# Residual sums shared between VectorE and GpSimd, the small product of the norm moved to VectorE, and a new order of all operations

## The chip, the cores and the metric

The kernel runs on one core of a Trainium2 chip. The metric is the device time of one execution in microseconds, the median of several runs. The engines are named as in the profile: PE (TensorE, matmuls), DVE (VectorE), ACT (ScalarE), POOL (GpSimd) and SP (SyncE, which issues all DMAs here).

## What is computed

The input x has 2048 rows of 448 bf16 values. Two blocks follow one another:

```python
x  = A_x
h  = x + attn(layernorm(x) @ wqkv) @ wo       # 16 heads of 28, causal window of 8 keys at steps of 2
y  = layernorm(h)
g  = gelu(layernorm(y) @ w1)                  # its four quarters shifted by -1, +1, -2, +2 rows
x1 = y + shifted(g) @ w2
out = h + (x1 + gelu(layernorm(x1) @ w3) @ w4)
```

The last line is the one that matters here: h, which lies in `xin`, has to be added to every row of x1 at the end, beside x1 itself.

## The kernel before

**Tiles and stages.** The 2048 rows are 16 tiles of 128. For the first half they are worked on in 4 groups of 4 tiles (512 rows), t = 0 to 3. Each goes through N1 (LayerNorm of x), A1 (transposed input times wqkv), V (values), A2 (logits with S, their softmax), A3 (weights times values, by way of block-diagonal factors `bd_r`), O (times wo, plus x: h), B1 (the two norms of h in one step, times w1, gelu) and M (its matmuls). The second half works in 5 units of 2, 4, 4, 4 and 2 tiles, u = 0 to 4: B2 (times w2, plus y: x1, called `xb`), T (LayerNorm of x1, made into `lntm` and turned by a transposing DMA into `actT`), W3 (times w3, gelu into `h3T`) and B3 (times w4, final sum, output). A letter with a number, such as T3 or W31, is a stage with its group or unit.

**Names.** `arena` is one large SBUF buffer; weights, q, k, g and the f32 rows `xb` lie in it, so that many rows of the profile have that name. `xin` holds x and then h (bf16). `lntm` are normalized rows, `mv` means and variances, `nm` negated means, `rs_x` variances and `rs_y` reciprocal standard deviations, `st` raw statistics, `pb`, `mx` and `ls` belong to the softmax, `ost` is the staging buffer of the output, `ps` a PSUM bank. `wo_s` holds wo, which comes in four DMAs.

**The end of a row.** y is never stored: y = h * rs_y - mean * rs_y. The B2 eviction (DVE, `scalar_tensor_tensor`) makes xb = h * rs_y + ps in f32. After T has read xb, the **residual sum** xb = xb + xin adds h (line 919-920, 16 times, one for each tile, on POOL). The **small product** mrs = nm * rs_y (line 547, four times, 128x4, on POOL) is the constant that is still missing in each row; the final eviction of B3 (line 944) computes ost = (ps + mrs) + xb on DVE. So neither the sum nor the product is needed before B3 of its tile.

**The order.** Every instruction is one of 858 operations, made by the phases and then sorted by a table of numbers, `ORDER` (line 22), which lists all of them: each engine executes its own operations in the order in which they stand there, strictly one after another. `OTHER` (line 53) lists the operations that take their alternative engine; most PSUM evictions have one (ACT or DVE). `arrange` (line 194) applies both and hands out buffers in that order from pools (8 PSUM banks, 3 `lntm`, 4 `actT`, 3 `bd_r`, 16 `h3T`, 5 `ost`): an operation waits for the last users of the buffer that it gets. `_emit_plan` (line 247) makes semaphore waits of the dependencies. POOL's queue holds set-up work, then `rs_y` as a power of `rs_x` where T takes it from there, the small products and the residual sums. SP's queue holds the DMAs: loads, copies of k and v between partitions (`arena<-arena`, `vw<-vt`), the transposes and the output.

Of the kernel before, what the change touches and what calls it, by code (L numbers as in the profile page):

```python
# [6 lines left out]
ALU = mybir.AluOpType  # L7
# [12 lines left out]
STAGE = '....'  # L20
ALONE = False
ORDER = """
# [29 lines left out]
"""  # L52
OTHER = """
91 94 114 187 188 501 507 549 550
"""
FULL = (4,)
FILL = (1, 1, 0, 0)
# [228 lines left out]
def bass_sequential_preLN__sliding_local_dilated__mixer_s_mlp__prompt_kernel(  # L286
# [16 lines left out]
    S = _Sched()  # L303
# [16 lines left out]
    with ExitStack() as es:  # L320
        def sb(name, shape, dt):
            return es.enter_context(nc.sbuf_tensor(name, shape, dt))
        AR = sb("arena", [128, A_END], BF16)
        xin = sb("xin", [128, NTL, D], BF16)
# [17 lines left out]
        rs_y = sb("rs_y", [128, 3, 2, NTL], F32)  # L342
        mrs = sb("mrs", [128, NTL], F32)
        nm = sb("nm", [128, 3, NTL], F32)
# [21 lines left out]
        def arv(off, parts, n):  # L366
            return AR[0:parts, off:off + n]
# [12 lines left out]
        xb = [arv(A_KV + i // 4 * KVB, 128, 4 * D * 2).bitcast(F32).rearrange("p (i d) -> p i d", d=D)[:, i % 4, :] for i in range(NTL)]  # L380
# [18 lines left out]
        def act(out_ap, in_ap, func, **kw):  # L399
            table = {ACT.Exp: "exp", ACT.Ln: "exp", ACT.Gelu_apprx_tanh: "gelu"}.get(func)  # L400
            return S.add("act", "activation", table=table, out=out_ap, in_=in_ap, func=func, **kw)
# [7 lines left out]
        def dve(meth, block=False, **kw):  # L409
            op = S.add("dve", meth, **kw)  # L410
            op.block = block
            return op

        def pool(meth, **kw):
            return S.add("pool", meth, **kw)
# [90 lines left out]
        def rstd(kind, i, m=4, summed=False, norms="v", how="p"):  # L506
            var = mv[:, kind, i:i + m, 1]
            by = 1.0 / D if summed else 1.0
            first = int(kind == 1)
            shifted_ = "a" in norms  # L510

            def power(k):
                S.add("pool", "tensor_tensor", out=rs_y[:, kind, k, i:i + m], in0=rs_x[:, kind, k, i:i + m], in1=mhalf[:, 0:m], op=ALU.pow)

            def power_act(k):
                act(rs_x[:, kind, k, i:i + m], var, ACT.Ln, scale=by * (1.0 + EPS * k), bias=epsilon[:, k:k + 1])
                act(rs_y[:, kind, k, i:i + m], rs_x[:, kind, k, i:i + m], ACT.Exp, scale=-0.5)

            def shift(k):
                if m == 1:  # L520
                    act(nmr[:, kind, i:i + 1], nm[:, kind, i:i + 1], ACT.Identity, scale=rs_y[:, kind, k, i:i + 1])
                else:
                    dve("tensor_tensor", out=nmr[:, kind, i:i + m], in0=nm[:, kind, i:i + m], in1=rs_y[:, kind, k, i:i + m], op=ALU.mult)

            if not summed and (shifted_ or kind == 1):
                dve("tensor_scalar", out=nm[:, kind, i:i + m], in0=mv[:, kind, i:i + m, 0], scalar1=-1.0, scalar2=None, op0=ALU.mult)
            if how == "a":
                power_act(first)
                if shifted_:
                    shift(first)  # L530
                if kind == 1:
                    power_act(0)
            else:
                if kind == 1:
                    dve("tensor_scalar", out=rs_x[:, kind, 1, i:i + m], in0=var, scalar1=by * (1.0 + EPS), scalar2=EPS * EPS, op0=ALU.mult, op1=ALU.add)
                    power(1)
                    if shifted_:
                        shift(1)
                if kind == 1 or summed:
                    dve("tensor_scalar", out=rs_x[:, kind, 0, i:i + m], in0=var, scalar1=by, scalar2=EPS, op0=ALU.mult, op1=ALU.add)  # L540
                else:
                    dve("tensor_scalar", out=rs_x[:, kind, 0, i:i + m], in0=var, scalar1=EPS, scalar2=None, op0=ALU.add)
                power(0)
                if kind != 1 and shifted_:
                    shift(0)
            if kind == 1:
                pool("tensor_tensor", out=mrs[:, i:i + m], in0=nm[:, 1, i:i + m], in1=rs_y[:, 1, 0, i:i + m], op=ALU.mult)

        CHUNK = (0, 128, 192, 320)

# [337 lines left out]
        def phase_B2(u):  # L888
# [28 lines left out]
            for n, i in enumerate(tiles):  # L917
                normalize(2, i, ln, n, xb[i], TURN["B2"][u], summed, norms[n])
            for i in tiles:
                S.add("pool", "tensor_tensor", out=xb[i], in0=xb[i], in1=xin[:, i, :], op=ALU.add).block = True  # L920
            b2_a[u] = transposed(ln, TURN["B2"][u], len(tiles))

        h3 = {}
# [129 lines left out]
```

## Time and profile before

| | us |
|---|---|
| median of 3 runs | 191.43 (191.26 to 191.53) |
| profiled execution | 191.99 |
| its span, first to last instruction | 190.3 |
| PE busy | 180.0 (95%), 2434 matmuls |
| DVE busy | 129.9 (68%) |
| ACT busy | 123.4 (65%) |
| POOL busy | 26.5 (14%) |

All instructions come from one line of the source, the emitting loop, so the profile's groups are told apart by the names of the tiles. A row of a timeline has the start, the length, the engine, the operation with output <- inputs, the number of instructions taken together and, in brackets, the idle time ahead of it with what ended it. A row SPq is a DMA's issue on SP's queue; the transfer goes on behind it. Matmul ends are modelled.

### The profile page before, as it was taken

What the parts mean: (1) busy time and instruction counts of PE and PEld (TensorE: products, weight loads), DVE (VectorE), ACT (ScalarE), POOL (GpSimd) and SP (SyncE); (2) the same over time, 40 slices, a digit from 0 to 9 for tenths busy, and PEclk for the clock granted to TensorE, in tenths of its full rate; (3) what the DMA queues carried; (4) which work ended last, traced back from release to release, by engine and by line L of the source; (5) the groups of instructions that cost most, each with busy time, mean ns of one, the idle gap of its engine ahead of it and who ended that gap; (6) DMA issues with size and microseconds to landing.
All of it is one profiled execution on the core that took longest, in us unless ns stands there. A gap on an engine that the chain in (4) does not pass through costs nothing.

```text
span 190.3 us, 5623 instructions
## 1 busy us (share of the span) xinstructions
PE 180.0 (95%) x2434; PEld 96.3 (51%) x2434; DVE 129.9 (68%) x226; ACT 123.4 (65%) x282; POOL 26.5 (14%) x61
## 2 busy tenths in 40 slices
PE   6699999897999989999989999999999999999994
PEld 2496433354443545565645535545444454455672
DVE  6999999999999999998998940099850006002203
ACT  3459999998999999999644897910256303650250
POOL 2250000000010000002205100181386002000000
DMA  5950254477407895796250060015044004000031
GB/s 147 339 193 3 44 110 110 78 174 158 103 3 114 160 272 225 136 331 134 50 113 0 5 134 0 3 30 108 0 91 119 0 0 112 19 3 0 17 109 48
DMA packets 36577, 18.06 MB, mean 95 GB/s; under 512 B 25304, under 2 KB 36040, under 8 KB 36552
## 3 DMA queue, kind: packets, MB, share of 16 engines
q1 hardware_dynamic: 36552, 17.70, 38.3%
q8 instruction: 19, 0.31, 0.7%
q14 instruction: 6, 0.05, 0.1%
HBM read 7.91 MB, written 1.84 MB: 51 GB/s over the span
## 4 chain that ended last, share of the span: by engine, by line
PE 56%; DVE 22%; ACT 11%; DMA 5%; SPq 2%; issue 2%; DVEq 0%; ACTq 0%
PE ps L1011 56%; DVE qk_r L1011 6%; DVE lntm L1011 5%; DVE bd_r L1011 4%; DMA arena<-in_A_wqkv_dram 3%; ACT lntm L1011 3%; SPq L1011 2%; DMA wo_s<-in_A_wo_dram 2%; ACT arena L1011 2%; DVE arena L1011 1%; ACT xin L1011 1%; DVE mx L1011 1%; DVE st L1011 1%; ACT h3T L1011 1%; ACT rs_x L1011 1%
## 5 line engine op out<-in xcount | busy, mean ns | idle before, releaser
L1011 PE MATMUL ps<-actT,arena 64*128 64x512 bf16 (+1 forms) x756 | 69.4, 329 | 0.9 <-ACT h3T L1011 0.4
L1011 ACT ACTIVATE h3T<-ps 128x512 bf16<-128x512 f32 (+1 forms) x70 | 30.8, 518 | 41.2 <-PE ps L1011 41.0
L1011 PEld LDWEIGHTS ps<-actT,arena 64*128 64x128 bf16 x756 | 37.3, 94 | 28.5 <-PE ps L1011 2.1
L1011 PE MATMUL ps<-arena,h3T 64*128 64x448 bf16 (+2 forms) x434 | 44.9, 343 | 0.4 <-DVE arena L1011 0.3
L1011 DVE SCALAR_TENSOR_TENSOR ost<-ps,mrs,arena 128x448 bf16<-128x448 f32 (+1 forms) x17 | 10.8, 650 | 40.6 <-PE ps L1011 40.6
L1011 ACT ACTIVATE arena<-ps 128x512 bf16<-128x512 f32 (+3 forms) x63 | 31.5, 541 | 3.7 <-PE ps L1011 3.2
L1011 PEld LDWEIGHTS ps<-arena,h3T 64*128 64x128 bf16 (+1 forms) x434 | 22.9, 94 | 20.0 <-DVE arena L1011 0.7
L1011 DVE TENSOR_TENSOR qk_r<-arena 128x4096 bf16<-128x4096 bf16 (+1 forms) x16 | 32.0, 2013 | 0.3 <-PE ps L1011 0.3
L1011 DVE TENSOR_TENSOR bd_r<-arena,bmask 80x2048 bf16<-80x2048 bf16 x16 | 19.8, 1270 | 0.1
L1011 POOL TENSOR_TENSOR arena<-arena,xin 128x448 f32<-128x448 f32 x16 | 17.1, 1086 | 14.8 <-DVE lntm L1011 14.8
L1011 DVE TENSOR_SCALAR lntm<-arena,mv,rs_y 128x512 bf16<-128x512 f32 x14 | 8.9, 679 | 12.2 <-ACT rs_y L1011 11.7
L1011 PE MATMUL ps<-wo_s,actT 64*128 64x448 bf16 x128 | 14.8, 350 | 1.1 <-DMA wo_s<-in_A_wo_dram 1.0
L1011 PE MATMUL ps<-w_s,arena 64*128 64x448 bf16 (+1 forms) x128 | 14.2, 350 | 0.1
L1011 PE MATMUL ps<-actT,w_s 64*112 64x512 bf16 x112 | 13.4, 378 | 0.0
L1011 ACT ACTIVATE actT<-ps 128x512 bf16<-128x512 f32 (+2 forms) x18 | 11.2, 653 | 3.2 <-PE ps L1011 3.2
L1011 PE MATMUL ps<-arena,actT 64*128 64x448 bf16 x112 | 13.2, 350 | 0.1
L1011 ACT ACTIVATE lntm<-xin,nm 128x448 bf16<-128x448 bf16 x16 | 10.5, 662 | 3.6 <-DVE nm L1011 3.6
L1011 POOL TENSOR_TENSOR mrs<-nm,rs_y 128x4 f32<-128x4 f32 x4 | 1.5, 387 | 71.9 <-ACT rs_y L1011 70.1
L1011 DVE SCALAR_TENSOR_TENSOR arena<-xin,rs_y,ps 128x448 f32<-128x448 bf16 x16 | 10.4, 667 | 0.0
L1011 DVE BATCH_NORM_STATS2 st<-xin 128x6 f32<-128x448 bf16 x16 | 9.2, 611 | 0.9 <-DMA xin<-in_A_x_dram 0.9
L1011 PEld LDWEIGHTS ps<-wo_s,actT 64*128 64x128 bf16 x128 | 5.6, 94 | 7.6 <-PE ps L1011 1.5
L1011 PEld LDWEIGHTS ps<-actT,w_s 64*112 64x112 bf16 x112 | 7.0, 127 | 4.7 <-DMA actT<-lntm 0.4
(70 smaller groups left out, 158.0 us busy)
## 6 DMA issues: line engine op xcount, KB each, us to landing
arena<-in_B_w_dram SPq DMA_DIRECT2D x2, 896.0 KB, 6.5
out_dram<-ost SPq DMA_DIRECT2D x15, 112.0 KB, 2.0
arena<-in_B_w_dram SPq DMA_DIRECT2D x2, 784.0 KB, 5.7
vw<-vt SPq DMA_DIRECT2D x4, 320.0 KB, 3.8
vw<-vt SPq DMA_DIRECT2D x4, 256.0 KB, 3.6
arena<-in_A_wqkv_dram SPq DMA_DIRECT2D x2, 448.0 KB, 4.7
xin<-in_A_x_dram SPq DMA_DIRECT2D x2, 448.0 KB, 7.2
xin<-in_A_x_dram SPq DMA_DIRECT2D x3, 224.0 KB, 5.9
```

Of the source, the lines that this page charges most:

```text
L1011: inst = getattr(eng, meth)(**kw)
```

## The change

1. The residual sum is no longer bound to POOL: it has DVE as its alternative engine. `OTHER` gives 9 of the 16 sums to DVE; 7 stay on POOL (two of T0, two of T1, one of T2, two of T3).
2. The small product is issued on DVE, all four times.
3. Four evictions that `OTHER` gave to the alternative engine are swapped for four neighbours of the same kind.
4. `ORDER` is another permutation of the same 858 operations. No matmul, DMA or eviction is added or taken away: PE has 2434 matmuls, SP 79 DMAs and ACT 244 operations as before; POOL goes from 57 operations to 44, DVE from 216 to 229.

```diff
 ORDER = """
-29 0 6 7 1 2 30 31 8 48 49 50 51 9 53 54 52 11 10 60 61 58 59 32 55 56 57 62 63 64 65 39 40 41 42 43 44 45 46 47 87 89
...
+7 0 1 5 6 3 39 40 41 42 43 44 45 8 48 49 2 9 53 50 51 52 54 46 47 11 10 58 29 60 59 61 87 30 55 56 57 32 62 63 89 90
...
 OTHER = """
-91 94 114 187 188 501 507 549 550
+88 96 113 187 188 498 501 549 550 614 615 683 684 686 754 755 815 816
 """
...
             if kind == 1:
-                pool("tensor_tensor", out=mrs[:, i:i + m], in0=nm[:, 1, i:i + m], in1=rs_y[:, 1, 0, i:i + m], op=ALU.mult)
+                dve("tensor_tensor", out=mrs[:, i:i + m], in0=nm[:, 1, i:i + m], in1=rs_y[:, 1, 0, i:i + m], op=ALU.mult)
...
             for i in tiles:
-                S.add("pool", "tensor_tensor", out=xb[i], in0=xb[i], in1=xin[:, i, :], op=ALU.add).block = True
+                both = dict(out=xb[i], in0=xb[i], in1=xin[:, i, :], op=ALU.add)
+                S.add("pool", "tensor_tensor", alts=[("dve", [("tensor_tensor", both)])], **both)
```

**POOL, from the end of the set-up to the end.** Sums are `arena<-arena,xin`, small products `mrs<-nm,rs_y`, powers `rs_y<-rs_x,mhalf`; brackets show the engine whose semaphore is waited for. Before:

```order
L1011 TENSOR_TENSOR mrs<-nm,rs_y 128x4 [waits sem_act]
L1011 TENSOR_TENSOR rs_y<-rs_x,mhalf 128x4 [waits sem_dve]
L1011 MEMSET arena 128x4x2
L1011 TENSOR_TENSOR mrs<-nm,rs_y 128x4 [waits sem_dve]
L1011 TENSOR_TENSOR arena<-arena,xin 128x448
L1011 TENSOR_TENSOR mrs<-nm,rs_y 128x4 [waits sem_act]
L1011 TENSOR_TENSOR arena<-arena,xin 128x448 x3
L1011 TENSOR_TENSOR mrs<-nm,rs_y 128x4 [waits sem_act]
L1011 TENSOR_TENSOR arena<-arena,xin 128x448 x2
L1011 TENSOR_TENSOR arena<-arena,xin 128x448 [waits sem_dve]
```

And now:

```order
L1012 MEMSET arena 128x4x2
L1012 TENSOR_TENSOR arena<-arena,xin 128x448 [waits sem_dve]
L1012 TENSOR_TENSOR rs_y<-rs_x,mhalf 128x4 [waits sem_dve]
L1012 TENSOR_TENSOR arena<-arena,xin 128x448 [waits sem_dve]
L1012 TENSOR_TENSOR arena<-arena,xin 128x448 x2
L1012 TENSOR_TENSOR rs_y<-rs_x,mhalf 128x4 [waits sem_dve]
L1012 TENSOR_TENSOR rs_y<-rs_x,mhalf 128x2 [waits sem_dve]
L1012 TENSOR_TENSOR arena<-arena,xin 128x448 x3
```

The first sum, of T0, moved ahead of the power of T1; the three behind that power are one of T1, the other of T0 and one more of T1 (released by `lntm` rows of T1 on DVE); nothing in the queue waits for ACT any more, and the three last (two of T3, one of T2) stand behind the powers of T3 and T4.

**SP, around the load of wo, in the stage A2 of the second group.** Before:

```order
L1011 DMA_TRANSPOSE actT<-lntm 128x16x128 [waits sem_dve]
L1011 DMA wo_s<-in_A_wo_dram 28x4x448
L1011 DMA arena<-arena 128x3x16
L1011 DMA wo_s<-in_A_wo_dram 28x4x448 x3
L1011 DMA vw<-vt 80x4x512
```

And now:

```order
L1012 DMA_TRANSPOSE actT<-lntm 128x16x128 [waits sem_dve]
L1012 DMA wo_s<-in_A_wo_dram 28x4x448 x2
L1012 DMA arena<-arena 128x3x16
L1012 DMA wo_s<-in_A_wo_dram 28x4x448
L1012 DMA arena<-arena 64x3x16 [waits sem_act]
L1012 DMA wo_s<-in_A_wo_dram 28x4x448
L1012 DMA vw<-vt 80x4x512
```

A second small copy, of k columns, moved in between the third and the fourth part of wo, and it waits for ACT.

**PE, at the end of W32 (`actT,arena` ahead of it) and the start of W33.** B32 is `arena,h3T`; `dsem_turn` is the wait for a transposing DMA. Before:

```order
L1011 MATMUL ps<-actT,arena 128x512 x11
L1011 MATMUL ps<-actT,arena 128x512 [waits dsem_turn1,sem_act]
L1011 MATMUL ps<-actT,arena 128x512 x7
L1011 MATMUL ps<-actT,arena 128x512 [waits sem_act]
L1011 MATMUL ps<-actT,arena 128x512 x7
L1011 MATMUL ps<-actT,arena 128x512 [waits sem_pe]
L1011 MATMUL ps<-actT,arena 128x512 x5
```

And now:

```order
L1012 MATMUL ps<-arena,h3T 128x448 [waits sem_act]
L1012 MATMUL ps<-arena,h3T 128x448 x13
L1012 MATMUL ps<-arena,h3T 128x448 [waits sem_act]
L1012 MATMUL ps<-arena,h3T 128x448 x13
L1012 MATMUL ps<-arena,h3T 128x448 [waits sem_act]
L1012 MATMUL ps<-arena,h3T 128x448 x27
L1012 MATMUL ps<-actT,arena 128x512 [waits dsem_turn3,sem_dve]
L1012 MATMUL ps<-actT,arena 128x512 x7
```

Before, W33 began right behind W32; now 56 matmuls of B32 stand ahead of its first group. On DVE, the six sums of T1, T2 and the first of T3 stand ahead of the last `lntm` of T3; the sums of T1 and T2 stood on POOL beside them.

56 rows, old and new, of the table ORDER are left out of this document.

## The prediction

> **What bounds the kernel now.** I read the busy shares first, then busy time by stretch, and last the timelines of the stretches where PE is not full. From the page, the shares:
>
> ```profile
> PE 180.0 (95%) x2434; PEld 96.3 (51%) x2434; DVE 129.9 (68%) x226; ACT 123.4 (65%) x282; POOL 26.5 (14%) x61
> ```
>
> PE is busy for 180.0 of 190.3 us, and the change touches no matmul. So 190.3 - 180.0 = 10.3 us are all that such a change can reach. The stretches of 20 us (columns: stretch, length, then the busy us of PE, PE's weight loads, DVE, ACT and POOL with their instructions):
>
> ```profile
> 30.00:50.00 20.00, 18.08 (x334) 8.70 (x330) 19.54 (x23) 18.29 (x50) 0.00 (x0) 1.00 0.52 109
> 50.00:70.00 20.00, 18.90 (x432) 9.13 (x430) 19.85 (x30) 19.70 (x47) 0.73 (x1) 1.00 0.65 126
> 70.00:90.00 20.00, 19.80 (x248) 11.17 (x246) 19.36 (x41) 19.14 (x45) 0.86 (x1) 1.00 0.75 219
> 90.00:110.00 20.00, 19.44 (x316) 11.02 (x318) 18.50 (x35) 12.10 (x25) 4.80 (x8) 1.00 0.21 45
> 110.00:130.00 20.00, 19.30 (x191) 9.49 (x188) 8.19 (x18) 12.71 (x24) 4.62 (x5) 1.00 0.28 56
> 130.00:150.00 20.00, 20.00 (x197) 9.28 (x194) 9.80 (x22) 8.47 (x16) 9.22 (x9) 1.00 0.25 59
> 150.00:170.00 20.00, 20.00 (x212) 10.10 (x209) 3.00 (x5) 6.76 (x13) 1.04 (x1) 1.00 0.13 31
> ```
>
> The granted clock is 1.00 in all of them. From 30 to 110 DVE is nearly full and PE loses 1.92, 1.10, 0.20 and 0.56 us, then 0.70; the other 5.8 of the 10.3 lie before 30 and after 170, in the load and the drain. From 130 on PE is full and DVE half empty: work may be given to DVE there for nothing, as long as no matmul comes to wait for it.
>
> **Step 1, the load of wo.** The first rows are SP's DMA issues, then one of the chain, then PE:
>
> ```profile
> 38.14 0.63 SPq L1011 DMA_DIRECT2D arena<-arena  x1
> 38.82 1.48 SPq L1011 DMA_DIRECT2D wo_s<-in_A_wo_dram  x3
> ```
> ```profile
> 39.90 4.17 DMA wo_s<-in_A_wo_dram
> ```
> ```profile
> 44.11 0.93 PE L1011 MATMUL ps<-wo_s,actT 64*128 64x448 bf16 x8 [0.95 <-DMA wo_s<-in_A_wo_dram]
> ```
>
> The fourth part of wo is issued at 39.90 and lands 4.17 later, and PE stands until then. The new order puts one more small copy (64x3x16) ahead of it; such a copy takes 38.82 - 38.14 = 0.68 of SP's queue, and it waits for an ACT copy besides. The price lies between 0, if SP comes there earlier, and somewhat over 0.68, if that ACT copy is late; I take the queue time, **+0.6**. DVE behind it is full until 90 (19.85 and 19.36 of 20), so the loss lasts till there.
>
> **Step 2, the statistics of T1, 88 to 92.** DVE there:
>
> ```profile
> 88.89 0.17 DVE L1011 TENSOR_SCALAR rs_x<-mv 128x4 f32<-128x4 f32 x1
> 88.97 0.68 DVE L1011 TENSOR_REDUCE mx<-ls 128x64 f32<-128x512 f32 x1
> 90.26 0.69 DVE L1011 TENSOR_TENSOR pb<-ls,mx 128x512 bf16<-128x512 f32 x1 [0.61 <-ACT mx L1011]
> ...
> 92.40 3.25 DVE L1011 TENSOR_TENSOR bd_r<-arena,bmask 80x2048 bf16<-80x2048 bf16 x2
> ...
> 96.03 1.21 DVE L1011 TENSOR_TENSOR bd_r<-arena,bmask 80x2048 bf16<-80x2048 bf16 x1
> ...
> 102.41 0.67 DVE L1011 SCALAR_TENSOR_TENSOR arena<-xin,rs_y,ps 128x448 f32<-128x448 bf16 x1
> ...
> 104.34 0.94 DVE L1011 TENSOR_SCALAR nm<-mv 128x4 f32<-128x4 f32 x1
> ```
>
> The reduction moves ahead of four small aggregations, so its 0.61 of waiting goes. But the lntm behind pb waits for POOL's power of rs_x (1.02, next rows), and only pb's 0.69 now lies over it: about 0.4 of waiting stays. Gain 0.2; the small product, new on DVE at this place, costs 0.15 (the row of nmr below). **-0.05**.
>
> **Step 3, POOL beside DVE, 92 to 106.** POOL's rows, and behind them DVE's lntm of T0:
>
> ```profile
> 89.14 1.02 POOL L1011 TENSOR_TENSOR rs_y<-rs_x,mhalf 128x4 f32<-128x4 f32 x1 [32.22 <-DVE rs_x L1011]
> ...
> 92.40 1.03 POOL L1011 TENSOR_TENSOR arena<-arena,xin 128x448 f32<-128x448 f32 x1
> 102.09 0.20 POOL L1011 TENSOR_TENSOR mrs<-nm,rs_y 128x4 f32<-128x4 f32 x1 [8.66 <-ACT rs_y L1011]
> 102.24 3.02 POOL L1011 TENSOR_TENSOR arena<-arena,xin 128x448 f32<-128x448 f32 x3
> ```
> ```profile
> 74.36 1.00 DVE L1011 TENSOR_SCALAR lntm<-arena,nm,rs_y 128x512 bf16<-128x512 f32 x2
> ```
>
> At 92.40 a residual sum and a bd_r product start together. Two bd_r take 3.25, where one alone takes 1.21: the second ends at 95.65 and is 1.14 behind the first, so the first held DVE for 2.11, 0.90 too long. At 104.34 the 128x4 nm takes 0.94 beside the third sum of the row of 102.24; its like takes 0.17 (rs_x at 88.89): 0.77 too long. Both lie on the chain that feeds PE. The sums stand there because POOL's queue is in order and each sits behind a small product that waits for ACT (8.66 above). With the products on DVE the T0 sum that T0's lntm releases near 75 (last row) runs there, and the other three run straight behind the power, at about 96 to 100. So the first bd_r is free (-0.90) and nm is free. What is uncertain is where the new first one (tile of 609) falls: it is released by the last lntm of T1, and the last bd_r of A33 is the next instruction on DVE. Its price lies between 0 (DVE first, POOL waits) and +0.90 (the pair as at 92.40); I take +0.2, since behind it DVE works on PSUM operands, and such an instruction beside POOL's sums at 102.41 took 0.67, the mean of its kind. Steps 1 to 3 up to O3: +0.6 - 0.05 - 0.90 + 0.2 = **-0.15**. The Trainium skill, page "SBUF — State Buffer", section "Who interferes with whom", says that a DVE instruction with two SBUF inputs contends with a GpSimd instruction that reads SBUF, and that one with at most one SBUF input, outside the two-port modes, does not; the 2.11 of bd_r agrees, and so does the 0.67 at 102.41.
>
> **Step 4, W31.** ACT first, then PE:
>
> ```profile
> 108.62 1.28 ACT L1011 ACT_TABLE_LOAD   x1
> 109.91 2.56 ACT L1011 ACTIVATE h3T<-ps 128x512 bf16<-128x512 f32 x5
> ```
> ```profile
> 106.14 4.51 PE L1011 MATMUL ps<-actT,arena 64*128 64x512 bf16 x40
> 111.05 4.82 PE L1011 MATMUL ps<-actT,arena 64*128 64x512 bf16 x42 [0.40 <-ACT h3T L1011]
> ...
> 123.12 1.49 PE L1011 MATMUL ps<-arena,h3T 64*128 64x448 bf16 x14
> 124.44 1.68 PE L1011 MATMUL ps<-w_s,arena 64*128 64x448 bf16 x16
> 125.96 1.50 PE L1011 MATMUL ps<-arena,h3T 64*128 64x448 bf16 x14
> 127.75 6.79 PE L1011 MATMUL ps<-arena,h3T 64*128 64x448 bf16 x70 [0.29 <-DVE arena L1011]
> ```
>
> ACT's chain nm, squares, table, first h3T starts 0.77 earlier from step 3, so the eviction at 109.91 comes some 0.9 earlier. PE's stall: a group of 14 shows 1.49 and its successor starts after 1.32, so the modelled end is 0.17 late; 106.14 + 4.51 - 0.17 = 110.48, and 0.57 is lost until 111.05. **-0.57**. What is next late there is none up to 115: PE then runs without a gap.
>
> **Step 5, B2 and B31.** By the same reckoning 125.96 + 1.32 = 127.28, and 0.47 is lost until 127.75, behind DVE's evictions. DVE reached them late because of T2's lntm:
>
> ```profile
> 123.34 3.17 DVE L1011 TENSOR_SCALAR lntm<-arena,mv,rs_y 128x512 bf16<-128x512 f32 x4 [11.71 <-ACT rs_y L1011]
> ...
> 136.79 3.10 DVE L1011 TENSOR_SCALAR lntm<-arena,mv,rs_y 128x512 bf16<-128x512 f32 x5 [0.54 <-POOL rs_y L1011]
> ```
>
> Four take 3.17 beside two POOL sums; five at 136.79, with one sum beside, take 3.10. In the new order no POOL sum is left there, and an eviction stands ahead of the lntm. **-0.47**.
>
> **Step 6, the nine sums on DVE.** Prices, from the groups of instructions:
>
> ```profile
> L1011 POOL TENSOR_TENSOR arena<-arena,xin 128x448 f32<-128x448 f32 x16 | 17.1, 1086 | 14.8 <-DVE lntm L1011 14.8
> ```
> ```profile
> L1011 DVE SCALAR_TENSOR_TENSOR arena<-xin,rs_y,ps 128x448 f32<-128x448 bf16 x16 | 10.4, 667 | 0.0
> L1011 DVE TENSOR_TENSOR nmr<-nm,rs_y 128x4 f32<-128x4 f32 x1 | 0.2, 151 | 0.0
> ```
>
> No row has the sum on DVE. The nearest is the eviction of the same shape to f32, 0.667, which I take as 0.65; below it lies the lntm of the same source (step 5: five in 3.10, 0.62 each, one of them held up), above it POOL's own 1.086 and, the dearest TENSOR_TENSOR of DVE with two SBUF operands that is of like size, bd_r alone at 1.21. The Trainium skill, page "VectorE: DVE Perf Modes", section "The TRN2 errata", measures an fp32 tensor_tensor of N elements at (N+151)/0.96 ns, an estimate of 0.62 us for this one, by which the sum would stand as it does. Six sums stand on DVE ahead of T3's last lntm: 6 x 0.65 + 0.15 for a small product = 4.05. T3's transposing DMA (first row) was issued at 139.45; the second row is PE's work around it.
>
> ```profile
> 139.45 1.97 SPq L1011 DMA_TRANSPOSE actT<-lntm  x1
> ```
> ```profile
> 134.38 13.98 PE L1011 MATMUL ps<-actT,arena 64*128 64x512 bf16 x128
> ```
>
> The transpose lands 4.3 after its issue, the median of the 11 transposes:
>
> ```profile
> actT<-lntm SPq DMA_TRANSPOSE x11, 4.3
> ```
>
> Now: 139.45 + 4.05 - 1.2 (steps 1 to 5) = 142.3, landing 146.6. W33's first group, in before behind 98 of the 128 matmuls (134.38 + 98 x 0.108 = 145.0), is in the new order behind four more groups of 14: 145.0 + 4 x 1.32 - 1.2 = 149.1. So 2.5 are to spare, and the sums cost **0**. The three later sums on DVE have its empty time as cover (3.00 busy in 150 to 170). Were the cover gone, each sum would cost its 0.65. The four evictions that trade engines keep each engine's count and shapes: 0, and at most one eviction's length (0.667) either way, were PE to wait for one. The start I leave as it is: PE's first matmul waits for a weight load that is issued as before.
>
> **The sum.** -0.15 - 0.57 - 0.47 = -1.2. The profiled execution took 191.99 (1.7 around its span), so its like would take 190.8; the median of the runs is 0.56 below that execution, 191.43, and goes to **190.2**. With the bounds of steps 1 and 3 (0 to +0.9 in place of +0.2, 0 to 0.7 in place of 0.6) this case holds from 189.4 to 191.0.
>
> **Rivals.**
>
> *The sums make T3 late (slower).* Place: DVE from 123 to 147, where the new sums take two SBUF operands, as bd_r does, while POOL's first T3 sum is released by the first of T3's four lntm. If the pair locks as at 92.40, that sum holds DVE for up to 1.03; and if a sum on DVE costs bd_r's 1.21, six cost 6 x 0.56 = 3.4 more. It decides when T3's transpose is issued over 2.5 later than I reckon, at 144.8, that is from 0.90 a sum with the lock, (2.5 - 1.03) / 6 over 0.65; from there PE waits one for one. At its full price 3.4 + 1.03 - 2.5 = 1.9: 192.1. For it: the 2.11 of bd_r, and that most of DVE's 9.80 us of 130 to 150 lie ahead of 139.89, where T3's lntm end, with one gap of 0.54 there. Against it: the 0.667 of the eviction. The rule that step 3 cites from the Trainium skill ("SBUF — State Buffer", "Who interferes with whom") speaks for this rival and against this change. Chance 0.23.
>
> *The collision only moves (same).* The first sum behind the power meets the last bd_r in full (+0.7 on my 0.2), and one of the two stalls of steps 4 and 5 stays: -1.2 + 0.7 + 0.5 = 0, 191.4. For it: last lntm and bd_r are neighbours on DVE. Against it: PE has other matmuls queued at that place. Chance 0.17.
>
> *More goes than I count (faster).* PE loses 1.92 and 1.10 between 30 and 70; if the new order feeds it there a third better, -1.0 more: 189.2. For it: DVE and PE are reordered there too. Against it: DVE is busy 19.54 and 19.85 of 20, so that order alone finds no room. Chance 0.1.
>
> **How the numbers follow.** Forecast 0.5, rivals 0.23, 0.17, 0.1. About 0.2% (0.4 us) is what a measurement can tell from no change. Faster: the forecast and the third rival, 0.6; same 0.17; slower 0.23. The range leaves out half of the third rival (0.05) and, for what lies beyond its full price, half of the first (0.12): 189.2 to 192.1.
>
> **What would show it.** Right: wo's last landing at 44.7 and PE's wait there near 1.5; POOL's T0 sum at 75; no bd_r over 1.3; nm under 0.2; no gap near 111 and 127; the sums on DVE at 0.6 to 0.7; PE full from 130. Wrong: a gap ahead of W33 near 149, a DVE sum over 1.0, or a bd_r of 2 us at 97.

## The result and the profile after

The changed kernel takes **190.11 us** (median of 4 runs, 189.32 to 190.29) against 191.48 for the kernel before (191.26 to 191.75): a ratio of **0.9923, 95% interval 0.9905 to 0.9942**. Beside the first experiments the same code came to 189.56 and 0.9900 (0.9872 to 0.9929). It is faster, by 1.4 to 1.9 us. The profiled execution took 190.29, its span is 188.3. From its page, the busy shares and the chain that ended last:

```profile
PE 180.3 (96%) x2434; PEld 99.1 (53%) x2434; DVE 133.1 (71%) x239; ACT 123.1 (65%) x282; POOL 16.8 (9%) x48
PE 79%; DVE 10%; ACT 5%; DMA 3%; issue 1%; SPq 0%; ACTq 0%
```

PE has the same 180 us of work and DVE 3.2 more. What was left to win was PE's idle time; by stretches of 20 us (PE's busy time is the third number):

```profile
30.00:50.00 20.00, 19.09 (x346) 8.99 (x344) 19.73 (x22) 18.58 (x49) 0.00 (x0) 1.00 0.44 86
50.00:70.00 20.00, 18.93 (x422) 9.15 (x420) 19.84 (x29) 19.68 (x47) 0.00 (x0) 1.00 0.73 175
70.00:90.00 20.00, 19.12 (x242) 11.16 (x238) 18.90 (x42) 18.90 (x43) 1.51 (x2) 1.00 0.68 183
90.00:110.00 20.00, 19.93 (x326) 11.04 (x326) 18.52 (x40) 13.58 (x29) 4.72 (x4) 1.00 0.32 49
110.00:130.00 20.00, 20.00 (x204) 10.84 (x202) 7.46 (x15) 10.89 (x21) 0.00 (x0) 1.00 0.29 57
```

From 90 to 130 PE is idle for 0.07 instead of 1.26; the chain says the same in one row, 1110 matmuls on end to the last eviction:

```profile
90.16 95.62 PE ps L1012 x1110
```

POOL's timeline shows where its sums went, and DVE's what they do to it there:

```profile
74.47 1.26 POOL L1012 TENSOR_TENSOR arena<-arena,xin 128x448 f32<-128x448 f32 x1 [62.47 <-DVE lntm L1012]
89.76 1.03 POOL L1012 TENSOR_TENSOR rs_y<-rs_x,mhalf 128x4 f32<-128x4 f32 x1 [14.02 <-DVE rs_x L1012]
96.65 3.94 POOL L1012 TENSOR_TENSOR arena<-arena,xin 128x448 f32<-128x448 f32 x3 [5.87 <-DVE lntm L1012]
```
```profile
90.36 0.69 DVE L1012 TENSOR_TENSOR pb<-ls,mx 128x512 bf16<-128x512 f32 x1 [0.69 <-ACT mx L1012]
...
92.62 3.49 DVE L1012 TENSOR_TENSOR bd_r<-arena,bmask 80x2048 bf16<-80x2048 bf16 x3 [0.20 <-ACT arena L1012]
...
96.49 1.22 DVE L1012 TENSOR_TENSOR bd_r<-arena,bmask 80x2048 bf16<-80x2048 bf16 x1
...
103.60 0.17 DVE L1012 TENSOR_SCALAR nm<-mv 128x4 f32<-128x4 f32 x1
```

Three bd_r in a row take 3.49, so none is held (two took 3.25 before); nm takes 0.17 instead of 0.94. At 96.49 DVE's last bd_r starts 0.16 ahead of POOL's sum and keeps its 1.22; it is POOL that pays, 3.94 for three sums that took 3.02 before (102.24). At 92.40, before, both started together and DVE paid 0.90. The Trainium skill says on the page "SBUF — State Buffer", section "Who interferes with whom", that the order of issue decides which of the two is blocked; the rows of 96.49 agree.

What the change added to DVE, by groups:

```profile
L1012 DVE TENSOR_TENSOR arena<-arena,xin 128x448 f32<-128x448 f32 x9 | 5.4, 616 | 0.0
L1012 DVE TENSOR_TENSOR mrs<-nm,rs_y 128x4 f32<-128x4 f32 x4 | 0.6, 153 | 0.0
```

5.4 + 0.6 us of work. PE's row of W33, 148.34, carries no wait, and neither does the row of B31 ahead of it, where the gap of 127 was:

```profile
127.17 5.47 PE L1012 MATMUL ps<-arena,h3T 64*128 64x448 bf16 x56
...
148.34 1.04 PE L1012 MATMUL ps<-actT,arena 64*128 64x512 bf16 x8
```

One meeting of DVE and POOL is left, and it costs nothing: beside POOL's last three sums (143.10, 3.39 long) T4's two lntm take 2.43, where two of T3's take 0.97 at 139.06, but PE has no gap between 130 and 170.

```profile
143.16 2.43 DVE L1012 TENSOR_SCALAR lntm<-arena,mv,rs_y 128x512 bf16<-128x512 f32 x2 [0.81 <-POOL rs_y L1012]
```

In front of 90 the picture is not what I forecast. SP's issues at the load of wo, the chain there, and two rows of PE:

```profile
38.71 0.60 SPq L1012 DMA_DIRECT2D wo_s<-in_A_wo_dram  x1
39.35 0.63 SPq L1012 DMA_DIRECT2D arena<-arena  x1
40.02 0.58 SPq L1012 DMA_DIRECT2D wo_s<-in_A_wo_dram  x1
```
```profile
40.02 3.41 DMA wo_s<-in_A_wo_dram
```
```profile
43.48 0.93 PE L1012 MATMUL ps<-wo_s,actT 64*128 64x448 bf16 x8 [0.60 <-DMA wo_s<-in_A_wo_dram]
...
73.08 0.72 PE L1012 MATMUL ps<-wo_s,actT 64*128 64x448 bf16 x5 [0.75 <-issue]
```

O0 starts at 43.48, 0.63 earlier than before and not 0.6 later. And in the middle of O2 PE stands for 0.75 with no wait that the profile shows. By 87 neither is left to see: the group of 42 matmuls `arena,h3T` starts at 87.28, 87.06 before.

### The profile page after: what moved, and what is told of

Same layout as the page of the kernel before. It is cut to its first block, busy times and chain, and to the rows that moved or that the text cites. A ratio compares the mean times of both kernels' runs of the same rounds, so it can differ in the third digit from the quotient of the medians.

```text
span 188.3 us, 5624 instructions
## 1 busy us (share of the span) xinstructions
PE 180.3 (96%) x2434; PEld 99.1 (53%) x2434; DVE 133.1 (71%) x239; ACT 123.1 (65%) x282; POOL 16.8 (9%) x48
## 4 chain that ended last, share of the span: by engine, by line
PE 79%; DVE 10%; ACT 5%; DMA 3%; issue 1%; SPq 0%; ACTq 0%
PE ps L1012 79%; DVE bd_r L1012 4%; ACT arena L1012 2%; DVE lntm L1012 2%; DMA wo_s<-in_A_wo_dram 2%; ACT xin L1012 2%; DVE qk_r L1012 2%; DMA xin<-in_A_x_dram 1%; DVE st L1012 1%; ACT vt L1012 0%; DVE ls L1012 0%; DVE bmask L1012 0%; ACT ls L1012 0%; DVE mx L1012 0%; ACT actT L1012 0%
## 5 line engine op out<-in xcount | busy, mean ns | idle before, releaser
L1012 PEld LDWEIGHTS ps<-actT,arena 64*128 64x128 bf16 x756 | 38.1, 94 | 26.9 <-PE ps L1012 2.9
L1012 PEld LDWEIGHTS ps<-arena,h3T 64*128 64x128 bf16 (+1 forms) x434 | 24.6, 94 | 17.6 <-PE ps L1012 0.5
L1012 DVE TENSOR_TENSOR bd_r<-arena,bmask 80x2048 bf16<-80x2048 bf16 x16 | 18.8, 1216 | 0.3 <-ACT arena L1012 0.2
L1012 POOL TENSOR_TENSOR arena<-arena,xin 128x448 f32<-128x448 f32 x7 | 8.6, 1248 | 68.3 <-DVE lntm L1012 68.3
L1012 PE MATMUL ps<-arena,actT 64*128 64x448 bf16 x112 | 12.1, 350 | 0.1
L1012 PEld LDWEIGHTS ps<-actT,w_s 64*112 64x112 bf16 x112 | 7.5, 127 | 4.2 <-ACT h3T L1012 0.3
L1012 PEld LDWEIGHTS ps<-w_s,arena 64*128 64x128 bf16 (+1 forms) x128 | 6.1, 94 | 6.1 <-PE ps L1012 0.5
```

The lines of the kernel that those rows point to most:

```text
L1012: inst = getattr(eng, meth)(**kw)
```

## The experiments

All are held against the kernel before on the same chip. Theory A was that order and engines work only together; B that the engines are the gain. After the first four runs A was narrowed to C: what counts is where POOL's sums meet DVE, and POOL's queue alone decides that; D, its rival, sees the gain in the order of PE, DVE and SP.

**The changed kernel again**, unedited.

> The changed kernel as it is, on the chip of the next three runs, so that they have something to be held against. The gaps of PE named in the prediction (44, 96, 111, 126) come out as in its first profile: a ratio of 0.990 to 0.994. Open is the gap of 0.75 us in the middle of O3's predecessor O2 (at 72.3), for which the profile names no wait: if it belongs to the code, it is there again; if it is an accident of one execution, it is gone and the span is 0.7 shorter.

Measured: 189.56, ratio 0.9900 (0.9872 to 0.9929). The gap in O2 is there again in the profiled execution, 1.02 us, and that execution took 190.84 while the other five took 189.26 to 189.76. The four later variants in the new order, with nearly the same PE code, do not have it in their profiles. So it belongs to some executions, and both profiles of this kernel happened to catch it. In both, w3's load is just ending at the time, and the DMA queue of instructions moves two packets between 69 and 75, one in those four variants. That PE waits for its own code there is not shown: the profile of one variant in the old order (T1's sums moved, below) has two such packets as well, and no stand.

**Old order, new engines.** The order of before, `OTHER` with the nine sums, the product on DVE:

```diff
-91 94 114 187 188 501 507 549 550
+91 94 114 187 188 501 507 549 550 614 615 683 684 686 754 755 815 816
...
-                pool("tensor_tensor", out=mrs[:, i:i + m], in0=nm[:, 1, i:i + m], in1=rs_y[:, 1, 0, i:i + m], op=ALU.mult)
+                dve("tensor_tensor", out=mrs[:, i:i + m], in0=nm[:, 1, i:i + m], in1=rs_y[:, 1, 0, i:i + m], op=ALU.mult)
...
-                S.add("pool", "tensor_tensor", out=xb[i], in0=xb[i], in1=xin[:, i, :], op=ALU.add).block = True
+                both = dict(out=xb[i], in0=xb[i], in1=xin[:, i, :], op=ALU.add)
+                S.add("pool", "tensor_tensor", alts=[("dve", [("tensor_tensor", both)])], **both)
```

> The order of before, with the nine sums and the four products on DVE. Theory A (order and engines only work together): POOL no longer meets bd_r at 92 to 94 or nm at 104, which is worth up to 0.9 + 0.6, but the old order puts five sums of 0.62 on DVE between 123 and 139, T3's transpose slips by about 3 us where 1.3 were to spare, and PE waits about 1.8 ahead of W33: 191.5 to 193. Theory B (the engines are the gain, the order is free): 189.9 to 190.5.

Measured: 192.49, ratio 1.0050 (1.0029 to 1.0071): slower. The time is in A's range, but the loss is not at A's place. W33 has no gap; PE loses between 90 and 110:

```profile
90.00:110.00 20.00, 18.17 (x304) 10.09 (x300) 18.98 (x33) 11.33 (x23) 5.63 (x4) 1.00 0.20 41
```
```profile
90.01 1.51 DVE L1012 TENSOR_TENSOR pb<-ls,mx 128x512 bf16<-128x512 f32 x1 [0.61 <-ACT mx L1012]
91.44 1.71 DVE L1012 TENSOR_SCALAR lntm<-arena,mv,rs_y 128x512 bf16<-128x512 f32 x2
93.07 1.00 DVE L1012 TENSOR_SCALAR nm<-mv 128x4 f32<-128x4 f32 x1
```

PE loses 1.83 there instead of 0.56. With the products gone from POOL's queue nothing holds its sums back, and they run from 89.93 on, into pb (1.51 instead of 0.69), two lntm (1.71 instead of 0.99) and nm (1.00 instead of 0.17). The bd_r behind them are late, but hardly held.

**New order, old engines.** The reverse: `pool(...)` for the product again, and the nine numbers taken out of `OTHER`.

> The new order, with all sums and products on POOL. Theory A: POOL's queue has the products in it again, but they stand where nothing waits for them; the sums meet DVE's small operations of 103 to 108 and T2's lntm at 126, up to 0.8 + 1.0, of which PE has slack for most: 190.2 to 191.0. Theory B (the engines are the gain): back to 191.2 to 191.7.

Measured: **189.63, ratio 0.9896 (0.9873 to 0.9919)**: as fast as the changed kernel, and faster than A's 190.2 to 191.0, since the meetings that A priced do not come. B is out: on this order, which engine runs the sums and products makes no difference that can be measured. POOL, with all sixteen sums:

```profile
96.50 3.94 POOL L1012 TENSOR_TENSOR arena<-arena,xin 128x448 f32<-128x448 f32 x3 [5.94 <-DVE lntm L1012]
...
126.14 5.01 POOL L1012 TENSOR_TENSOR arena<-arena,xin 128x448 f32<-128x448 f32 x5 [19.72 <-DVE lntm L1012]
```

The sums stand at the same 96.5 with the products on POOL, because one product has run long before (76.29) and the next two stand behind the sums (106.08). Five more run behind T2's last lntm instead of beside it.

**The small copy behind the fourth part of wo**, in the changed kernel:

```diff
-... 460 20 21 240 22 352
-23 167 168 459 ...
+... 460 20 21 240 22 23 352
+167 168 459 ...
```

> The changed kernel with the small copy moved behind the fourth part of wo, as in before. If the copy costs its time in SP's queue, as my step 1 has it, that part is issued 0.65 earlier, at 39.4, and O0 starts up to 0.5 earlier (PE is busy until 42.9): 189.6 to 190.0 with PE's gap at 43 nearly gone. If the landing is set by the transfers and not by the issue, the landing stays within 0.2 of 43.4 and the time within 0.2.

Measured: 189.40, 0.9889 (0.9861 to 0.9917), not apart from the changed kernel's 0.9900. It is the second case: SP issues the fourth part at 39.07 instead of 40.02, but it lands 4.2 behind its issue instead of 3.4, and O0 starts at 43.29 instead of 43.48. PE's row for O0, with another name in the bracket, the load of its weights (PEld), and the row of ACT that the bracket means:

```profile
43.29 0.93 PE L1012 MATMUL ps<-wo_s,actT 64*128 64x448 bf16 x8 [0.68 <-ACT actT L1012]
```
```profile
43.28 0.49 PEld L1012 LDWEIGHTS ps<-wo_s,actT 64*128 64x128 bf16 x8 [0.80 <-DMA wo_s<-in_A_wo_dram]
```
```profile
42.69 0.60 ACT L1012 ACTIVATE actT<-ps 128x512 bf16<-128x512 f32 x1
```

The weight load still waits for wo. ACT's eviction happens to end at the same 43.29; in the changed kernel the same eviction (42.96, 0.60 long) ends at 43.56, after O0 has begun, so that O0 does not wait for it. An issue 0.95 earlier brought a landing 0.2 earlier; what holds the transfer back, no run shows.

**Old order, only POOL's queue changed.** PE, DVE, ACT and SP keep theirs to the last instruction; in `ORDER` five sums move:

```diff
-... 548 549 550 399 ... 514 552 588 ... 664 551 586 ...
+... 548 549 550 551 552 399 ... 514 588 ... 664 586 ...
...
-... 520 615 518 ... 807 614 647 ... 525 612 613 685 684 810 ... 719 686 755 ...
+... 520 518 ... 807 647 ... 525 686 612 613 614 615 685 684 810 ... 719 755 ...
```

> The kernel before with nothing but POOL's queue in another order: T0's two sums behind T0's lntm (at 75), T1's four behind the first T2 sum (at 126); PE, DVE, ACT and SP keep theirs, and products and sums stay on POOL. Theory C (the gain of 92 to 128 is POOL's sums no longer meeting DVE's bd_r, nm and lntm): PE's gaps at 96 (0.78), 110 (0.59) and 126 (0.47) go, less what is late next: 189.7 to 190.5. Rival D (the gain is in the order of PE, DVE and SP): 191.2 to 191.6, with gaps of like size at those places.

Measured: **189.28, ratio 0.9901 (0.9881 to 0.9921)**. That is the whole gain of the change, from one queue of the old order, and 0.4 more than C gave it. POOL, and PE's two stretches:

```profile
74.80 2.27 POOL L1011 TENSOR_TENSOR arena<-arena,xin 128x448 f32<-128x448 f32 x2 [18.07 <-DVE lntm L1011]
...
123.77 6.99 POOL L1011 TENSOR_TENSOR arena<-arena,xin 128x448 f32<-128x448 f32 x7 [2.18 <-DVE lntm L1011]
```
```profile
90.00:110.00 20.00, 20.00 (x324) 11.35 (x322) 18.31 (x38) 13.56 (x28) 0.66 (x3) 1.00 0.21 43
110.00:130.00 20.00, 20.00 (x204) 11.02 (x202) 8.24 (x18) 11.08 (x21) 6.43 (x8) 1.00 0.31 65
```

No sum runs on POOL between 77 and 123, and PE has no gap between 90 and 130. D is out as the reason: the old order of PE, DVE and SP has the whole gain. The reverse, POOL's sums at their old places in the new order, was not run, so what the new order of the others would be worth without the move is open.

**The two moves by themselves:** first the upper hunk alone (551 and 552), then the lower alone (686, 614 and 615).

> The kernel before with only T0's two sums moved on POOL, behind T0's lntm. Theory C: the sum that held bd_r at 92.4 is gone from there, and PE's gap at 96 (0.78) with it; the other two gaps (0.59 and 0.47) stay, since T1's sums still meet nm and T2's lntm: about 0.8 less than before, 190.4 to 190.9. If one collision hides the other, so that it takes both moves: 191.1 to 191.5.

Measured: 190.00, ratio 0.9927 (0.9900 to 0.9955), 1.4 us less by the ratio, 1.2 by the medians; more than I gave it. POOL has one sum fewer in front of 104, so nm is free as well, and the gap ahead of W31 goes with that at 96. T2's lntm are still held:

```profile
103.77 0.17 DVE L1011 TENSOR_SCALAR nm<-mv 128x4 f32<-128x4 f32 x1
```
```profile
122.08 3.17 DVE L1011 TENSOR_SCALAR lntm<-arena,mv,rs_y 128x512 bf16<-128x512 f32 x4 [11.51 <-ACT rs_y L1011]
```

> The kernel before with only T1's four sums moved on POOL, behind the first T2 sum, after T2's lntm. Theory C: nm at 104 and T2's lntm at 123 are alone, the gaps of 0.59 and 0.47 go, that at 96 stays: about 1.0 less, 190.2 to 190.7. With the run above the two moves then add up to the 2.0 of both. Otherwise 191.1 to 191.5.

Measured: 190.30, ratio 0.9952 (0.9931 to 0.9973), 0.9 us less. The two bd_r take 3.25 as before, and PE has its gap behind them; T2's lntm run free, in 1.92:

```profile
91.80 3.25 DVE L1011 TENSOR_TENSOR bd_r<-arena,bmask 80x2048 bf16<-80x2048 bf16 x2
...
122.04 1.92 DVE L1011 TENSOR_SCALAR lntm<-arena,mv,rs_y 128x512 bf16<-128x512 f32 x4 [11.57 <-ACT rs_y L1011]
```
```profile
96.69 0.42 PE L1011 MATMUL ps<-bd_r,vw 80*32 80x64 bf16 x32 [0.56 <-DVE bd_r L1011]
```

The gap ahead of W31 goes in both. What each move is worth can be read within one execution, from the start of the 14 matmuls `arena,h3T` ahead of the bd_r groups (94.62 before) to the start of W32 (134.38): PE takes 39.76 before, 38.39 with T0's sums moved, 38.60 with T1's and 37.91 with both, which is 1.37, 1.16 and 1.85 less. Taken from start to start against the run without them, the three gaps are 0.69 at 96, 0.72 ahead of W31 and 0.47 at 126, so that 0.69 + 0.72 = 1.41, 0.72 + 0.47 = 1.19 and 1.88 were to go. The ratios, each good to about 0.5 us, say 1.4, 0.9 and 1.9.

**Old order, only the product on DVE.** One line, `pool(...)` to `dve(...)`.

> The kernel before with the four small products on DVE and nothing else. POOL's queue then holds back no sum for ACT: they run from 90 to 97, beside A33's four bd_r. Theory C: up to three of these are held for 0.9, against the 0.57 and 0.47 of the later gaps: 191.4 to 192.4. Rival (a free POOL queue is the gain, as step 3 has it): 189.9 to 190.6.

Measured: **194.97, ratio 1.0190 (1.0170 to 1.0210)**, 3.6 us slower, worse than either theory. POOL and DVE:

```profile
94.35 6.35 POOL L1011 TENSOR_TENSOR arena<-arena,xin 128x448 f32<-128x448 f32 x3 [0.36 <-DVE lntm L1011]
```
```profile
91.99 1.02 DVE L1011 TENSOR_TENSOR mrs<-nm,rs_y 128x4 f32<-128x4 f32 x1
92.93 1.33 DVE L1011 TENSOR_SCALAR lntm<-arena,mv,rs_y 128x512 bf16<-128x512 f32 x1
94.19 3.18 DVE L1011 TENSOR_TENSOR bd_r<-arena,bmask 80x2048 bf16<-80x2048 bf16 x2
...
97.76 2.05 DVE L1011 TENSOR_TENSOR bd_r<-arena,bmask 80x2048 bf16<-80x2048 bf16 x1
```

The product itself takes 1.02 beside a sum, the next lntm 1.33, two bd_r are 0.8 too long, and each of POOL's sums takes 2.1. The wait for ACT in POOL's queue, which I had counted as the fault, was in the old order what kept most sums out of this stretch.

Not all of the 3.6 us are collisions, though. PE waits 1.20 and 2.02 for two of the bd_r, and directly behind these waits its granted clock, the third number from the end in a row by stretches, is 0.50 for some 3 us:

```profile
100.00:101.00 1.00, 1.00 (x36) 0.60 (x30) 1.00 (x2) 0.47 (x1) 0.70 (x1) 0.50 1.15 218
```
```profile
99.86 0.62 PE L1011 MATMUL ps<-bd_r,vw 80*32 80x64 bf16 x32 [2.02 <-DVE bd_r L1011]
100.41 1.68 PE L1011 MATMUL ps<-w_s,arena 64*128 64x448 bf16 x8
```

Eight matmuls that took 0.93 before take 1.68, and from the third bd_r group to the fourth PE needs 3.48 (99.86 to 103.34) instead of 2.10 (97.30 to 99.40). So about 1.4 of the 3.6 go to the clock and some 2.2 to the collisions, which is still over the 192.4 of theory C. All four executions of this variant have a mean clock of 0.991, those of every other kernel here 0.999 or 1.000.

**PE's gap at the softmax, in the old order:**

```diff
-... 149 343 150 151 133 249 355 256 258 362 356 357 358 152 ... 335 345 346 ...
+... 149 343 150 151 133 249 355 256 258 362 356 357 358 345 346 152 ... 335 ...
```

> The kernel before with PE's 14 matmuls of the next group (A1) put ahead of the 16 that wait for pb, where PE stands 0.88 at 34.3; the new order does the like. If that gap is a loss of its own: 190.6 to 191.0. If the chain behind it runs over DVE, which is full there, PE only waits elsewhere until 70: 191.3 to 191.6.

Measured: 191.24, ratio 1.0007 (0.9987 to 1.0027): no change. PE's wait for pb is gone, and one of the same length, for ACT and ahead of the next matmuls of that group, has taken its place:

```profile
36.64 1.04 PE L1011 MATMUL ps<-actT,arena 64*128 64x512 bf16 x8 [0.69 <-ACT arena L1011]
```

**Each of six sums three times**, in the changed kernel: two more instructions of the same shape ahead of it, written to `qk_r`, which is no longer in use.

> The changed kernel with each of the six sums ahead of T3's last lntm preceded by two more of the same size into a buffer that is no longer used: 12 x 0.6 = 7.2 us more on DVE between 126 and 141. By step 6 the first 2.5 to 2.8 are hidden and the rest is paid at W33: about 4.5 more than the changed kernel, 193.5 to 194.5. If T3 is not what counts there, PE waits earlier, for banks that DVE evicts late, or hardly at all: under 192, or over 195.

Measured: 192.85, ratio 1.0078 (1.0055 to 1.0102), some 3.3 above the changed kernel; 4.5 were expected. PE:

```profile
126.18 5.47 PE L1013 MATMUL ps<-arena,h3T 64*128 64x448 bf16 x56
...
135.13 2.98 PE L1013 MATMUL ps<-actT,arena 64*128 64x512 bf16 x26 [1.76 <-DVE ost L1013]
138.67 6.22 PE L1013 MATMUL ps<-actT,arena 64*128 64x512 bf16 x56 [0.56 <-DVE ost L1013]
...
150.44 1.04 PE L1013 MATMUL ps<-actT,arena 64*128 64x512 bf16 x8 [0.26 <-DVE lntm L1013]
```

What is late first is B31's output: its PSUM banks are freed by evictions that stand behind the sums on DVE, and W32 waits for these banks, 1.76 and 0.56. T3 is late as well:

```profile
146.03 2.00 SPq L1013 DMA_TRANSPOSE actT<-lntm  x1
```

It lands 4.3 later, at 150.3, and W33 starts at 150.44. Its row shows only 0.26 of waiting because W32's waits had already used most of the time. Counted from B31's row (126.18 here, 127.17 in the changed kernel), T3's issue slipped by 5.8 and W33 by 3.1, so 2.7 were hidden, as the expectation had it. Its error is the 7.2: DVE is busy for 6.2 more (139.3 instead of 133.1), and some of that falls into its idle time.

**The two variants that were not slower, together:** new order, all sums and products on POOL, the copy behind wo.

> The new order with all sums and products on POOL and the small copy behind the fourth part of wo, the two variants of it that were not slower, together. If nothing before 90 binds but DVE, it is as the changed kernel, 189.2 to 189.7 (0.988 to 0.991); a gain would show below 189.0.

Measured: 189.78, ratio 0.9921 (0.9895 to 0.9946). No gain over the changed kernel; none of the variants is apart from it on the faster side.

## Why the prediction came out as it did

The time was right (190.2 against 190.11) and so was the sign. Not every step was, and that it came to within 0.1 is luck: two misses cancel, as the sum below shows.

*Step 1, +0.6 for the copy ahead of wo: wrong.* O0 came 0.63 earlier. PE waited 0.60 there instead of the 1.5 that was to show it. The step took time in SP's queue for time on the path, but the landing does not follow the issue: with the copy moved away the fourth part is issued 0.95 earlier and lands 0.2 earlier. It also read one transfer of one execution: the 4.17 from issue to landing was the longest of the seven profiles of the old order, where it goes down to 3.66; the two profiles of the unedited new order have 3.41 and 3.47. And where O0 starts is not felt later: the 42 matmuls `arena,h3T` start between 86.26 and 87.17 in the seven profiles of the old order and between 86.29 and 87.85 in the six of the new one.

*Step 2, -0.05: about right, by another way.* The wait ahead of pb did not go: it is 0.69 instead of 0.61, for ACT's `mx` and not for POOL's power, and the product took 0.153. From the four lntm that stand ahead of T1's statistics to pb, DVE needs 5.32 (85.04 to 90.36) instead of 5.44 (84.82 to 90.26).

*Step 3, POOL beside DVE: right in its places and wrong in its reason.* The 0.90 of bd_r and the 0.77 of nm went; the new meeting at 96.5 was paid by POOL, so its +0.2 was 0. Of the 0.90 on DVE, PE had lost 0.69, and these two errors of 0.2 cancel. But the sums did not come free because the products left POOL's queue. That alone costs 3.6 us in the old order (some 2.2 without the slower clock), and putting the products back costs nothing in the new one. The place of the sums in POOL's queue is the cause: in the old order it is by itself worth the whole gain. The prediction had read that part in the two listings of POOL's queue and then gave the credit to the wrong edit.

*Steps 4 and 5, -0.57 and -0.47: right.* Both gaps are gone (the first is 0.72 with the slower start behind it), each with the collision that it was traced to, in the run that moves just that.

*Step 6, nine sums on DVE for nothing: right.* A sum takes 0.616 (0.65 was taken), T3's transpose is issued at 141.18 (142.3 was reckoned), and W33 starts at 148.34 without a wait. The rival built on that place had a real mechanism and the wrong price for a sum: with each of the six sums three times, T3 is late and W33 starts 3.1 later. What both left out is W32, which in that run waits first, for banks behind `ost`.

*The sum.* Step 1 was 0.6 too high and nothing was set aside for the stand in O2, 0.75 in the first profile, that some executions have: the two about cancelled. In the second measurement, where only the profiled one of six executions ran above 189.8, the gain is 1.9, near the 1.88 of the three gaps alone, and the forecast would have been 0.6 too slow. The rival in which the collision only moves did not happen in the new order; it is what the old order with new engines does. The rival in which more goes found its place and gained nothing by it: PE is idle for 0.9 instead of 1.9 between 30 and 50, but for 0.9 instead of 0.2 between 70 and 90.

## What to carry to other kernels

An engine that is 14% busy and never on the critical path can still hold a full one, so look for instructions that take longer than their like, and then at what the neighbour was doing in those microseconds. In this kernel it was the place of the cheap work in its queue that paid, and not the engine it ran on: try to move such work within its own queue first, and only where something waits for the engine that it holds. Before a DMA's issue is moved, look whether its landing follows: here it did not. And before a wait is priced, look what the same engine would wait for next: in the run at the softmax the wait went and another of the same length took its place.

## What the hardware showed that I had not expected

How far the interference goes: a 128x4 product of 0.153 took 1.02, and POOL's sums took 2.1 each beside bd_r, so that three in a row ran at half their pace (6.35 instead of 3.02), while a bd_r took 2.05 instead of 1.21. And an instruction that starts 0.16 earlier keeps its full speed. PE's granted clock was 0.50 from 100 to 103 in the variant with the product on DVE, directly behind waits of 1.20 and 2.02, and the matmuls there took 1.68 instead of 0.93 for eight. PE's stand of 0.75 to 1.02 us inside O2, with no semaphore behind it, comes and goes between executions of the same program and is about as large as each of the effects measured here; what it waits for stays open.
